# Subtracting the block means from V on VectorE ahead of the mix, in place of a second matmul per column

## The chip, the cores and the metric

The kernel runs on one core of one Trainium2 chip. The metric is the device time of one execution in microseconds (us); less is better. A profile is one execution; its span is some 2 us shorter than the device time of the same execution. Engines are named as in the profile: PE is TensorE's matmuls, PEld its weight loads, DVE VectorE, ACT ScalarE, POOL GpSimd, SP SyncE. Names in the profile's lines: pm and pf are PSUM tiles; vst is V of the first mix as loaded, vcx V in the order that a mix reads, vbn its mean, bdv the block-diagonal P, vsf the mixed V; qr is a copy of q; un is the layer norm's result, w1sb and w2sb the MLP's weights, hr its hidden layer, and u what goes out.

## The reference, cut to what matters

The code is written out in short here, not word for word.

```python
# attention over 4 batches x 8 heads, 768 positions in 8 blocks of 96, head width 64
P = sort_net                               # 8 x 8 for each (batch, head)
for _ in range(5):
    P = ...                                # exp, rows and columns normalised in turn
k_sorted = einsum('bhij,bhjcd->bhicd', P, k_blocks)
v_sorted = einsum('bhij,bhjcd->bhicd', P, v_blocks)     # "the mix" of this text
attn = softmax(q_blocks @ k_sorted^T / 8)
x = attn @ v_sorted                        # then 2D Fourier mix, layer norm,
...                                        # and an MLP 512 -> 2048 -> 512 with two residuals
```

The kernel works with V less its mean over the 96 rows of a block. The mean goes through a small path of its own, in float32. Batches 0 and 1 are mixed together (the first mix), batches 2 and 3 together (the second mix).

## The kernel before

The rows of V lie on partitions, one for each (batch, head, block), 128 for two batches. For every one of the 64 columns of the head, one matmul has that column of V (96 rows and padding) as weights and a block-diagonal copy of P as the moving matrix. A second matmul into the same PSUM column takes off the mean.

```python
def v_sort(n):                      # first mix only: V in the order that the mix needs
    nc.vector.tensor_copy(vcx[...4 * n:4 * n + 4], vst[:, 24 * n:24 * n + 24, :]...)
    op("DVE", 0.6)

def vb_make(t, src):                # the mean, and its negative in 16 bits
    ...
    vbn[t] = const.tile([128, D], F16, name=f"vbn{t}")
    nc.vector.tensor_scalar(vbn[t], vb[:, 0, :], -1.0, None, op0=ALU.mult)
    ...

def v_mix(t, n):                    # n = 0..15: four columns
    bd = bdv16[t].rearrange("p g i -> p (g i)")
    ps = pm([128, 4, 128])
    for dd in range(4):
        d = 4 * n + dd
        nc.tensor.matmul(ps[:, dd, :], vcx[:, :, d], bd, start=True, stop=False)
        nc.tensor.matmul(ps[:, dd, :], vbn[t][:, d:d + 1].broadcast_to([128, 128]),
                         bd, start=False, stop=True)
    t = op("PE", 0.46)
    evac(vsb[0:96, :, 4 * n:4 * n + 4], ps[0:96]..., t, 512)   # PSUM to SBUF, on ACT or DVE
```

`op(engine, us)` computes nothing on the chip. It keeps an estimated clock for each engine while the program is being written, and these estimates decide which of several streams (attention, mix, Fourier transform, layer norm, MLP) writes its next piece, and whether ACT or DVE evacuates. A scheduler of the build then moves instructions within windows (64 instructions on PE, 12 on DVE and on ACT). So a figure given to `op` changes the order of instructions, and at times which of the two engines evacuates, but never what is computed.

The softmax here doesn't subtract the row's maximum and nothing guards it: scores larger than these inputs give would overflow.

Of the kernel before, what the change touches and what calls it, by code (L numbers as in the profile page):

```python
# [10 lines left out]
F16 = mybir.dt.float16  # L11
I32 = mybir.dt.int32
AF = mybir.ActivationFunctionType
ALU = mybir.AluOpType
# [6 lines left out]
D = 64  # L21
# [79 lines left out]
def kernel(  # L101
# [10 lines left out]
    nc = tc.nc  # L112
    cn = {n: nc.inline_tensor(a, name="k_" + n) for n, a in _consts().items()}

    const = ctx.enter_context(tc.tile_pool(name="const", bufs=1))
# [12 lines left out]
    def pm(shape, dtype=F32):  # L128
        cnt[0] += 1
        return pml.tile(shape, dtype, tag="pm", name=f"pm{cnt[0]}")  # L130

    def wt(shape, dtype, tag, bufs, nm=None):
        cnt[0] += 1
        return work.tile(shape, dtype, tag=tag, bufs=bufs,
                         name=f"{nm or tag}{cnt[0]}")
# [18 lines left out]
    def op(e, dur, after=0.0):  # L154
        t = max(clk[e], after) + dur
        clk[e] = t
        return t + LAT
# [5 lines left out]
    def evac(dst, src, after, n):  # L163
        da, dv = 0.22 + n / 1200.0, 0.15 + n / 960.0
        e = pick(after, da, dv)
        if e == "ACT":
            nc.scalar.copy(dst, src)  # L167
            return op(e, da, after)
        nc.vector.tensor_copy(dst, src)
        return op(e, dv, after)  # L170
# [41 lines left out]
    vcx = const.tile([128, 128, D], F16, name="vcx")  # L212
# [3 lines left out]
    def load_v(t):  # L216
        for g in range(2):
            start(nc.gpsimd.dma_start(
                vcx[:, 48 * g:48 * g + 48, :].rearrange(
                    "p (c r) d -> p c (r d)", r=3),  # L220
                vv[128 * t:128 * t + 128, :, g, :]))
# [15 lines left out]
    for n in range(NKS):  # L237
        t = const.tile([128, NB, 128], F16, name=f"ksb{n}")
# [19 lines left out]
    pwt = pw.rearrange("p i j -> p j i")  # L258

    def v_sort(n):  # L260
        nc.vector.tensor_copy(
            vcx[:, 0:BLK, :].rearrange("p (g c r) d -> p g c (r d)", g=2, r=3)[
                :, :, 4 * n:4 * n + 4],
            vst[:, 24 * n:24 * n + 24, :].rearrange(
                "p (c g r) d -> p g c (r d)", g=2, r=3))
        op("DVE", 0.6)

    def v_mean(psm, n, src=vcx):
        nc.tensor.matmul(  # L269
            psm.rearrange("p c d -> p (c d)"), idh,  # L270
            src[:, 8 * n:8 * n + 8, :].rearrange("p c d -> p (c d)"),
            start=(n == 0), stop=(n == 11))
        op("PE", 0.22)
# [3 lines left out]
    def q_copy(b, hp, after=0.0):  # L277
        hf, hl = divmod(hp, 2)
        q16 = qk["q", b, hf]
        qr = wt([128, 6, 2, D], F16, "qr", 2)  # L280
        nc.vector.tensor_copy(
            qr, q16[:, 2 * hl:2 * hl + 2].rearrange("p h r d -> p r h d"))
        qrs[b, hp] = (qr, op("DVE", 0.35, after))

    ph = []
    for it in range(5):
        if it == 0:
# [3 lines left out]
                op=ALU.subtract)  # L291
# [28 lines left out]
    for c in range(4):  # L320
        w = nc.gpsimd.dma_start(w1sb[:, c, :], w1v[:, c, :])
# [23 lines left out]
    psm = pm([128, 8, D])  # L345
# [5 lines left out]
    t = wt([128, H, NB, 16], F16, "bdk", 2)  # L351
    for hh in range(2):
# [5 lines left out]
            op=ALU.mult)  # L358
# [6 lines left out]
    def kq(b, hp):  # L365
        hf, hl = divmod(hp, 2)
        k16 = qk["k", b, hf]
        ks = ksb[kcnt[0] % NKS]
        kcnt[0] += 1
        for half in range(2):  # L370
            ps = pf([128, 3, 128])
            for r3 in range(3):
                r = 3 * half + r3
                for h2 in range(2):
                    nc.tensor.matmul(  # L375
                        ps[64 * h2:64 * h2 + 64, r3, :],
                        k16[:, 2 * hl + h2, r, :],
                        bdk[b][:, 2 * hp + h2].rearrange("p i c -> p (i c)"))
            t = op("PE", 0.2)
            t1 = evac(ks[:, :, 48 * half:48 * half + 48].rearrange(  # L380
                "p i (c r) -> p i c r", r=3),
                ps.rearrange("p r (i c) -> p i c r", c=16), t, 384)
        qr, tq = qrs[b, hp]
        ps = pf([128, 6, 128], F16)
        for r in range(6):
            nc.tensor.matmul(ps[:, r, :], qr[:, r].rearrange("p h d -> p (h d)"),  # L386
                             idh, is_transpose=True)
        t = op("PE", 0.35, tq)
        qt = wt([128, 6, 128], F16, "qt", 3)
        nc.vector.tensor_copy(qt, ps)  # L390
        t2 = op("DVE", 0.55, t)
        return ks, qt, max(t1, t2)
# [70 lines left out]
    vbn = {}  # L463

    def bdv_make():
        psv = pm([128, NB, 32])
        for i in range(NB):
            nc.tensor.matmul(psv[:, i, :], pv[:, i, :], idf[0:32, 0:32])
        for t in range(2):
            b32 = const.tile([128, 16, NB], F32, name=f"bdv32_{t}")  # L470
            nc.vector.tensor_tensor(
                b32, psv[:, :, 16 * t:16 * t + 16].rearrange("p i g -> p g i"),
                maskg[:, :, None].broadcast_to([128, 16, NB]), op=ALU.mult)
            b16 = const.tile([128, 16, NB], F16, name=f"bdv16_{t}")
            nc.scalar.copy(b16, b32)
            bdv32.append(b32)
            bdv16.append(b16)

    def vb_make(t, src):
        vb = const.tile([128, 2, D], F32, name=f"vb{t}")  # L480
        nc.vector.tensor_reduce(vb[:, 0, :], src.rearrange("p c d -> p d c"),
                                axis=AX.X, op=ALU.add)
        nc.vector.tensor_scalar(vb[:, 0, :], vb[:, 0, :], 1.0 / BLK, None,
                                op0=ALU.mult)
        vbn[t] = const.tile([128, D], F16, name=f"vbn{t}")
        nc.vector.tensor_scalar(vbn[t], vb[:, 0, :], -1.0, None, op0=ALU.mult)
        nc.vector.tensor_copy(vb[:, 1, :], vb[:, 0, :])
        vbs[t] = vb

    def v_mix(t, n):  # L490
        bd = bdv16[t].rearrange("p g i -> p (g i)")
        ps = pm([128, 4, 128])
        for dd in range(4):
            d = 4 * n + dd
            nc.tensor.matmul(ps[:, dd, :], vcx[:, :, d], bd, start=True,  # L495
                             stop=False)
            nc.tensor.matmul(ps[:, dd, :],  # L497
                             vbn[t][:, d:d + 1].broadcast_to([128, 128]),
                             bd, start=False, stop=True)
        t = op("PE", 0.46)  # L500
        evac(vsb[0:96, :, 4 * n:4 * n + 4],
             ps[0:96].rearrange("p d g -> p g d"), t, 512)

# [368 lines left out]
    def v1_gen():  # L872
        load_v(1)
        while (0, 0) not in uns:
            yield None
        ps = pm([128, 8, D])
        for n in range(12):
            v_mean(ps, n)
        vb_make(1, ps)
        op("DVE", 0.9, clk["PE"])  # L880
        while 1 not in attnd:
            yield None
        for n in range(16):
            v_mix(1, n)
            yield clk["PE"] + 0.6
        vmixed[0] = True
# [29 lines left out]
    def sc(kk):  # L916
        es = new_es()
        t0 = scores(*kk[:2], 0, es)
        t1 = scores(*kk[:2], 1, es)
        return kk + (es, [max(a, c) for a, c in zip(t0, t1)])  # L920
# [2 lines left out]
    k0 = {0: kq(0, 0)}  # L923
    for n in range(6, 12):
        v_mean(psm, n, vst)
    for n in range(4):
        v_sort(n)
    k0[0] = sc(k0[0])
    bdv_make()
    q_copy(0, 1)  # L930
    k0[1] = kq(0, 1)
    nc.scalar.copy(tkh, psk)
    vb_make(0, psm)
    k0[1] = sc(k0[1])
    load_qk(1, 0)
    for n in range(16):
        v_mix(0, n)
# [14 lines left out]
    add(1, a_gen())  # L952
    add(2, attn_gen(k0))
    add(3, v1_gen())
    add(4, mlp_gen())
    with ExitStack() as later:
# [42 lines left out]
```

## Time and profile before

The time before is 323.6 us (median of 3 runs, 322.8 to 323.98). From the page of the profile, the line of PE: busy us, share of the span, instructions.

```profile
PE 290.4 (90%) x2444; PEld 181.8 (57%) x2444; DVE 203.0 (63%) x454; ACT 122.6 (38%) x254; POOL 40.1 (12%) x73
```

PE is the busiest engine, but the average hides three stages. The chain that ended last shows the first one (columns: start us, us, what):

```profile
22.08 28.77 DMA q<-in_q_dram
51.56 1.15 PE pf L444 x12
```

One load, of q for batch 1, lies across the whole first mix (24 to 35 us) and releases the work at 51 us. Next, the busy time of each engine in stretches of the span:

```profile
core 0: us, PE busy (x) PEld busy (x) DVE busy (x) ACT busy (x) POOL busy (x), PEclk, DMA share, GB/s
80.00:86.00 6.00, 5.13 (x78) 4.31 (x72) 3.86 (x12) 4.37 (x10) 0.00 (x0) 1.00 0.83 128
86.00:100.00 14.00, 13.07 (x170) 10.46 (x169) 13.70 (x28) 12.11 (x25) 4.75 (x6) 1.00 0.04 4
100.00:110.00 10.00, 9.74 (x133) 8.41 (x133) 4.15 (x12) 9.93 (x22) 0.00 (x0) 1.00 0.51 78
110.00:125.00 15.00, 14.75 (x188) 10.49 (x186) 10.72 (x32) 9.92 (x24) 1.49 (x2) 1.00 0.41 61
125.00:314.00 189.00, 188.53 (x1201) 104.12 (x1200) 110.08 (x221) 45.09 (x91) 11.19 (x24) 1.00 0.15 43
```

The second mix runs from 82 to 107 us. From 86 to 100 us PE stands still for 0.9 of 14 us and DVE is busy for 13.7; ACT is busy for 12.1, and for 9.9 of the 10 us that follow. After 125 us PE is full: whatever PE saves before, or loses, appears at the end.

The groups that the change touches (line, engine, operation, operands, shape, count, busy us, mean ns, idle before them):

```profile
L495 PE MATMUL pm<-bdv,vcx 128*128 128x128 f16 x128 | 21.9, 267 | 1.0 <-DMA vcx<-k_dtab 0.5 <-ACT vsf L167 0.5
L497 PE MATMUL pm<-bdv,vbn 128*128 128x128 f16 x128 | 21.6, 237 | 0.0
L636 DVE TENSOR_TENSOR pmt<-r 128x1536 f16<-128x1536 f16 x8 | 7.4, 952 | 0.0
L261 DVE COPY vcx<-vst 128x1536 f16<-128x1536 f16 x4 | 2.0, 552 | 0.0
```

The mean ns of a matmul is its latency, and matmuls overlap. What one costs is read from the timeline, as the distance of the starts (columns: start us, us, engine, line, operation):

```profile
89.04 0.22 PE L497 MATMUL pm<-bdv,vbn 128*128 128x128 f16 x1
89.10 0.25 PE L495 MATMUL pm<-bdv,vcx 128*128 128x128 f16 x1
89.19 0.22 PE L497 MATMUL pm<-bdv,vbn 128*128 128x128 f16 x1
89.25 0.26 PE L495 MATMUL pm<-bdv,vcx 128*128 128x128 f16 x1
```

A pair starts every 0.148 us. The matmul with the column of V is followed after 0.09 us, the one with the mean after 0.06.

### The profile page before, as it was taken

To read this page: it belongs to the slowest core of one execution; us is meant where nothing else is said; L and a number is where in the kernel's file an instruction comes from. 1 tells how busy PE (TensorE), PEld (TensorE's weight loads), DVE (VectorE), ACT (ScalarE), POOL (GpSimd) and SP (SyncE) were. 2 spreads that over 40 slices of the span, in tenths; PEclk is the share of its full clock that TensorE was granted. 3 is DMA by queue.
4 is the path that set the end of the run, shared out by engine and by line. 5 is a ranking of instruction groups with operands and counts; after the bars stand their busy time and mean duration, and the time that the engine had idled before them with its cause. 6 is when DMAs were issued, how large, how long until landed. Compare 5 with 4: busy or idle time off the path is not lost.

```text
span 321.6 us, 5938 instructions
## 1 busy us (share of the span) xinstructions
PE 290.4 (90%) x2444; PEld 181.8 (57%) x2444; DVE 203.0 (63%) x454; ACT 122.6 (38%) x254; POOL 40.1 (12%) x73
## 2 busy tenths in 40 slices
PE   0389974699899999999999999999999999999995
PEld 0169853466777776455455656554664564554642
DVE  6795686888795656466495667644943662872831
ACT  2266481568789963012048843210460120110000
POOL 8320051013122010010003000100020010010000
PEclk9986995599999999999999999999999999999999
DMA  8999979971506070102111100021021120121002
GB/s 126 209 290 219 207 122 208 175 103 19 91 3 98 2 100 15 65 34 51 62 48 35 19 33 35 33 51 65 33 51 59 41 51 33 66 48 68 33 2 98
DMA packets 30131, 24.90 MB, mean 77 GB/s; under 512 B 15028, under 2 KB 25780, under 8 KB 30102
## 3 DMA queue, kind: packets, MB, share of 16 engines
q0 software_dynamic: 15552, 13.63, 27.3%
q1 hardware_dynamic: 14552, 10.89, 11.2%
q8 instruction: 19, 0.31, 0.4%
q14 instruction: 8, 0.07, 0.1%
HBM read 29.10 MB, written 6.29 MB: 110 GB/s over the span
## 4 chain that ended last, share of the span: by engine, by line
PE 70%; DMA 9%; ACT 9%; DVE 6%; issue 3%; POOL 2%; POOLq 0%; ACTq 0%
PE pm L802 26%; PE pm L785 24%; DMA q<-in_q_dram 9%; PE pf L749 7%; PE pf L444 4%; ACT ex L408 2%; PE pf L666 2%; PE pf L752 2%; PE pf L400 2%; ACT eb L424 1%; PE pf L375 1%; PE pf L386 1%; ACT vsf L167 1%; ACT un L714 1%; DVE eb L234 1%
## 5 line engine op out<-in xcount | busy, mean ns | idle before, releaser
L785 PE MATMUL pm<-ut,w1sb 128*128 128x384 f16 x512 | 92.5, 327 | 0.0
L802 PE MATMUL pm<-w2sb,hr 128*128 128x512 f16 x384 | 86.8, 379 | 0.0
L785 PEld LDWEIGHTS <-w1sb 128*128 128x128 f16 x512 | 49.8, 100 | 32.9 <-issue 1.2
L802 PEld LDWEIGHTS <-hr 128*128 128x128 f16 x384 | 37.3, 99 | 42.7
L794 ACT ACTIVATE hr<-pm 128x384 f16<-128x384 f32 x47 | 22.9, 493 | 99.1 <-PE pm L785 99.0
L790 DVE TENSOR_SCALAR hr<-pm 128x384 f16<-128x384 f32 x81 | 44.8, 555 | 20.7 <-PE pm L785 17.1
L811 DVE TENSOR_TENSOR u<-pm,u 128x512 f32<-128x512 f32 x24 | 16.5, 687 | 40.9 <-PE pm L802 40.9
L408 ACT ACTIVATE ex<-pf 96x384 f32<-96x384 f32 x64 | 28.2, 489 | 11.8 <-PE pf L400 11.6
L444 PE MATMUL pf<-vsf,eb 97*128 97x96 f16 x384 | 21.3, 211 | 5.5 <-DVE eb L421 4.5
L714 ACT ACTIVATE un<-u,nm,ny 128x512 f16<-128x512 f32 x20 | 15.6, 809 | 25.3 <-POOL nm L702 19.5
L698 POOL TENSOR_SCALAR mv<-mv 128x3 f32<-128x3 f32 x8 | 3.3, 417 | 173.5 <-DVE mv L760 173.5
L444 PEld LDWEIGHTS <-eb 97*128 97x128 f16 x384 | 19.5, 100 | 8.3 <-DVE eb L421 4.6
L424 ACT ACTIVATE eb<-ex,negone 96x384 f16<-96x384 f32 x38 | 23.1, 622 | 0.3
L495 PE MATMUL pm<-bdv,vcx 128*128 128x128 f16 x128 | 21.9, 267 | 1.0 <-DMA vcx<-k_dtab 0.5
L756 DVE SCALAR_TENSOR_TENSOR u<-r,pf 128x512 f32<-128x512 f16 x24 | 16.3, 681 | 9.5 <-DMA out_dram<-u 5.7
L497 PE MATMUL pm<-bdv,vbn 128*128 128x128 f16 x128 | 21.6, 237 | 0.0
L495 PEld LDWEIGHTS <-vcx 128*128 128x128 f16 x128 | 20.1, 173 | 1.3 <-issue 0.9
L497 PEld LDWEIGHTS <-vbn 128*128 128x128 f16 x128 | 17.4, 136 | 0.7 <-issue 0.7
L456 DVE TENSOR_TENSOR r<-pf,rz 128x384 f16<-128x384 f32 x32 | 17.1, 551 | 0.5
L759 DVE BATCH_NORM_STATS2 st<-u 128x6 f32<-128x512 f32 x24 | 16.5, 688 | 0.3
L167 ACT CAST vsf<-pm 96x512 f16<-96x512 f32 x18 | 14.3, 813 | 4.3 <-PE pm L497 4.0
L269 PE MATMUL pm<-vst,pack 128*128 128x512 f16 x12 | 4.2, 501 | 12.2 <-DMA vst<-in_v_dram 12.2
(103 smaller groups left out, 327.5 us busy)
## 6 DMA issues: line engine op xcount, KB each, us to landing
out_dram<-u SPq DMA_DIRECT2D x24, 256.0 KB, 2.0
k<-in_k_dram POOLq DMA_DIRECT2D x8, 384.0 KB, 8.2
q<-in_q_dram POOLq DMA_DIRECT2D x8, 384.0 KB, 9.4
w1sb<-in_moe_w_ch_dram POOLq DMA_DIRECT2D x4, 512.0 KB, 19.6
w2sb<-in_moe_w_ch_dram POOLq DMA_DIRECT2D x4, 512.0 KB, 25.1
vst<-in_v_dram POOLq DMA_DIRECT2D x2, 768.0 KB, 10.7
vcx<-in_v_dram POOLq DMA_DIRECT2D x2, 768.0 KB, 22.7
cs<-k_cs SPq DMA_DIRECT2D x1, 579.0 KB, 13.0
```

The costliest lines, as they stand in the source:

```text
L167: nc.scalar.copy(dst, src)
L408: nc.scalar.activation(ex.rearrange("p j (c r) -> p j c r", r=6), pss[h2][0:96].rearrange("p j (r c) -> p j c r", c=16), AF.Exp, scale=SCALE)
L424: nc.scalar.activation(ed, src, AF.Identity, bias=negone[0:96])
L444: nc.tensor.matmul(po[:, 65 * T:65 * T + 96], e[:, S * g + 256 * tt + 128 * n: S * g + 256 * tt + 128 * n + 128], vsf[:, vi:vi + 96], star ...
L495: nc.tensor.matmul(ps[:, dd, :], vcx[:, :, d], bd, start=True, stop=False)
L497: nc.tensor.matmul(ps[:, dd, :], vbn[t][:, d:d + 1].broadcast_to([128, 128]), bd, start=False, stop=True)
L714: nc.scalar.activation(un, ul[tt], AF.Identity, scale=y[:, tt:tt + 1], bias=nm[:, tt:tt + 1])
L749: nc.tensor.matmul(ps[:, c % 2::2], lh, dtab[:, c, :], start=(c == 0), stop=False, skip_group_check=True)
L785: nc.tensor.matmul(ps, w1sb[:, c, 128 * fc:128 * fc + 128], ut[:, c, :], start=(c == 0), stop=(c == 3))
L790: nc.vector.tensor_scalar(hr[:, fc, :], ps, 0.0, None, op0=ALU.max)
L794: nc.scalar.activation(hr[:, fc, :], ps, AF.Relu)
L802: nc.tensor.matmul(ps, hr[:, fc, 128 * tt:128 * tt + 128], w2sb[:, fc, :], start=(fc == 0), stop=(fc == 15))
```

## The change

The mean is taken off on VectorE. In the first mix the sort copy becomes a subtraction; in the second, four subtractions in place stand ahead of the mix. One matmul per column stays. The figures given to `op` change with it. In the opening sequence the subtractions have to follow the mean, so its order changes too.

```diff
--- before.py
+++ after.py
@@ -258,12 +258,25 @@
     pwt = pw.rearrange("p i j -> p j i")
 
     def v_sort(n):
-        nc.vector.tensor_copy(
+        nc.vector.tensor_tensor(
             vcx[:, 0:BLK, :].rearrange("p (g c r) d -> p g c (r d)", g=2, r=3)[
                 :, :, 4 * n:4 * n + 4],
             vst[:, 24 * n:24 * n + 24, :].rearrange(
-                "p (c g r) d -> p g c (r d)", g=2, r=3))
-        op("DVE", 0.6)
+                "p (c g r) d -> p g c (r d)", g=2, r=3),
+            vm3(0)[:, None, None, :].broadcast_to([128, 2, 4, 3 * D]),
+            op=ALU.subtract)
+        op("DVE", 0.9)
+
+    def v_center(n):
+        w = vcx[:, 24 * n:24 * n + 24, :].rearrange(
+            "p (c r) d -> p c (r d)", r=3)
+        nc.vector.tensor_tensor(
+            w, w, vm3(1)[:, None, :].broadcast_to([128, 8, 3 * D]),
+            op=ALU.subtract)
+        op("DVE", 0.9)
+
+    def vm3(t):
+        return vbn[t].rearrange("p r d -> p (r d)")
 
     def v_mean(psm, n, src=vcx):
         nc.tensor.matmul(
@@ -482,8 +495,9 @@
                                 axis=AX.X, op=ALU.add)
         nc.vector.tensor_scalar(vb[:, 0, :], vb[:, 0, :], 1.0 / BLK, None,
                                 op0=ALU.mult)
-        vbn[t] = const.tile([128, D], F16, name=f"vbn{t}")
-        nc.vector.tensor_scalar(vbn[t], vb[:, 0, :], -1.0, None, op0=ALU.mult)
+        vbn[t] = const.tile([128, 3, D], F16, name=f"vbn{t}")
+        nc.vector.tensor_copy(
+            vbn[t], vb[:, 0:1, :].broadcast_to([128, 3, D]))
         nc.vector.tensor_copy(vb[:, 1, :], vb[:, 0, :])
         vbs[t] = vb
 
@@ -492,12 +506,8 @@
         ps = pm([128, 4, 128])
         for dd in range(4):
             d = 4 * n + dd
-            nc.tensor.matmul(ps[:, dd, :], vcx[:, :, d], bd, start=True,
-                             stop=False)
-            nc.tensor.matmul(ps[:, dd, :],
-                             vbn[t][:, d:d + 1].broadcast_to([128, 128]),
-                             bd, start=False, stop=True)
-        t = op("PE", 0.46)
+            nc.tensor.matmul(ps[:, dd, :], vcx[:, :, d], bd)
+        t = op("PE", 0.25)
         evac(vsb[0:96, :, 4 * n:4 * n + 4],
              ps[0:96].rearrange("p d g -> p g d"), t, 512)
 
@@ -878,6 +888,8 @@
             v_mean(ps, n)
         vb_make(1, ps)
         op("DVE", 0.9, clk["PE"])
+        for n in range(4):
+            v_center(n)
         while 1 not in attnd:
             yield None
         for n in range(16):
@@ -923,14 +935,16 @@
     k0 = {0: kq(0, 0)}
     for n in range(6, 12):
         v_mean(psm, n, vst)
-    for n in range(4):
-        v_sort(n)
+    vb_make(0, psm)
     k0[0] = sc(k0[0])
     bdv_make()
+    for n in range(2):
+        v_sort(n)
     q_copy(0, 1)
     k0[1] = kq(0, 1)
     nc.scalar.copy(tkh, psk)
-    vb_make(0, psm)
+    for n in range(2, 4):
+        v_sort(n)
     k0[1] = sc(k0[1])
     load_qk(1, 0)
     for n in range(16):
```

## The prediction

> **What bounds the kernel now.** TensorE is busy 90% (page), but stages differ.
> (a) To 51 us the loads decide: in the chain of waits one piece of 28.8 us, the load of q for batch 1, lands at 50.9 us; DVE idles 4.0 us before it (waits, qr copy). The first mix (24 to 35 us) lies inside, with about 4 us of slack.
> (b) From 80 to 110 us (second mix) all three engines are full: by windows PE is busy 13.1 and DVE 13.7 of 14 us from 86 to 100, ACT 13.6 of 14 from 94 to 108.
> (c) From 125 to 318 us PE is busy 192.4 of 193 us: PE work saved, or idle added, before this shows in full at the end.
>
> **What the change does.** It removes 128 PE matmuls (64 per mix). By timeline a pair starts every 0.148 us at full clock, 0.213 at half clock (24 to 29 us). The Trainium skill ("TensorE: Matmul & The Clock Gate", Back-to-back issue gap and Part 1) gives 107 ns cold and 56 warm for one such matmul. The trace agrees cold; 0.148 is above two warm ones, so I estimate 0.06 to 0.1 us for the strided V load that stays. Saved: some 4 us of PE in each mix (3 to 5.5).
>
> It adds DVE work. The four sort copies (552 ns each, 128x1536 fp16) become subtractions; a tensor_tensor of that size takes 952 ns (pmt group). The skill ("VectorE: DVE Perf Modes", Mode 4×_2P) says tensor_tensor cannot use the fourfold mode; the two times agree. Four in-place subtractions come before the second mix: +3.5 us pipelined. The 16 vsf evacuations per mix stay at 0.8 us over two engines: no mix group below about 0.41 us, against 0.6 now.
>
> **Order.** DVE's built order is unchanged between the first mix and 79 us, with the waiting qr copy in place. The first mix starts about 1.5 us later (subtractions wait for the mean), takes 7 instead of 11 us, and its gain is swallowed by the wait for q: worth 0.
> In the second the subtractions stand between the mean (80.6 us) and the first mix matmul, among eb copies that PE's attention matmuls need. I expect the mix to start near 86.5 instead of 82, with about 2 us of new PE idle. DVE is then 1 to 2 us behind in a stage already full, and two vsf evacuations and some hr move to the full ACT. Most of the saved PE time turns into waits. Both orders join again near 138 us.
>
> **Time.** 4 saved, minus 2 idle at the start, minus about 1 more: -1 us. I predict 322.3 us, 80% range 318.5 to 326. Faster by over 2% 0.06, within 2% 0.91, slower by over 2% 0.03.
>
> **What would show it.** Chain: q still lands near 51 us. Groups: no vbn matmuls; subtractions 0.9 to 1.0 us each. Timeline: first second-mix matmul near 86 us; PE idle from 80 to 110 us up from 2.1 to 4 us or more; the first w2sb matmuls 0 to 2 us earlier than now (124.4); the tail unchanged.
>
> **What would make it wrong.** If q or V land sooner in the early stretch, the gain is 2 to 4 us larger. If subtractions run at one element per cycle (estimate 1.6 us each), DVE falls 3 us further behind: slower. If mlp work fills the stage, the full 4 to 5 us are won.

## The result, and the profile after

The time after is 320.16 us (median of 4 runs, 320.0 to 320.3), against 323.52 us for the kernel before (322.8 to 323.98). The ratio is 0.9896, with a 95% interval of 0.9882 to 0.991: 1.0% less time, which counts as the same at the threshold of 2%. Ratios in this text are taken from runs of both kernels in the same rounds; they need not be the ratio of the medians that are quoted.

The line of PE on the page after, and the same part of the chain:

```profile
PE 283.4 (89%) x2316; PEld 174.3 (55%) x2316; DVE 205.3 (64%) x453; ACT 124.6 (39%) x259; POOL 39.5 (12%) x73
```

```profile
23.44 27.57 DMA q<-in_q_dram
51.72 1.15 PE pf L457 x12
```

128 matmuls and 7 us of PE's busy time are gone, but the load of q still releases the work, 0.16 us later than before. The windows after:

```profile
80.00:86.00 6.00, 4.57 (x73) 3.54 (x69) 5.93 (x13) 4.65 (x10) 0.00 (x0) 1.00 0.86 130
86.00:100.00 14.00, 13.19 (x144) 10.30 (x143) 12.73 (x27) 12.91 (x26) 2.52 (x4) 1.00 0.01 2
100.00:110.00 10.00, 10.00 (x109) 7.49 (x107) 6.81 (x21) 9.95 (x24) 1.62 (x2) 1.00 0.57 80
110.00:125.00 15.00, 15.00 (x185) 10.29 (x183) 8.31 (x21) 9.88 (x24) 1.48 (x2) 1.00 0.43 63
125.00:314.00 189.00, 188.53 (x1218) 104.55 (x1215) 111.22 (x224) 45.15 (x91) 11.21 (x24) 1.00 0.16 46
```

Summed over the first four rows, PE's idle time is 2.31 us before and 2.24 after. The new idle time that the prediction expected isn't there: 0.6 us more before 86 us, and 0.6 less from 86 to 100. (From 80 to 110 us, where it looked for 4 us or more, it is 2.05 before and 2.24 after.) The groups after:

```profile
L509 PE MATMUL pm<-bdv,vcx 128*128 128x128 f16 x128 | 15.5, 268 | 2.4 <-issue 1.0 <-DVE vsf L169 0.6 <-DVE vcx L273 0.4
L273 DVE TENSOR_TENSOR vcx<-vcx,vbn 128x1536 f16<-128x1536 f16 x4 | 3.8, 942 | 0.0
L261 DVE TENSOR_TENSOR vcx<-vst,vbn 128x1536 f16<-128x1536 f16 x4 | 3.6, 947 | 0.0
```

The subtractions take 942 and 947 ns, as the tensor_tensor of the same shape did before. And the timeline of PE after, at the start of the second mix:

```profile
86.48 0.57 PE L509 MATMUL pm<-bdv,vcx 128*128 128x128 f16 x4 [0.43 <-DVE vcx L273]
86.89 0.81 PE L795 MATMUL pm<-ut,w1sb 128*128 128x384 f16 x4
87.54 0.49 PE L509 MATMUL pm<-bdv,vcx 128*128 128x128 f16 x4
...
90.66 1.24 PE L509 MATMUL pm<-bdv,vcx 128*128 128x128 f16 x12
```

The second mix starts 4.5 us later (81.94 before), as predicted, but PE works on other matmuls until then, and matmuls of the MLP (w1sb) fill the gaps between the groups of four. From a group of 12 (1.24 us) and one of 4 (0.49), the distance of two mix matmuls is about 0.75/8 = 0.094 us; in weight loads, twelve take 1.26 us, with starts 0.097 us apart. Against the pair's 0.148 that saves 0.051 us, times 64 columns 3.3 us in each mix.

To say where the gain arises, I cut the span at two marks that every version has: the end of the matmuls that sum the second mean, and the fourth of the output additions of the MLP. Here is the last group of the first mark and then the second mark, before and after:

```profile
78.09 1.24 PE L269 MATMUL pm<-vcx,pack 128*128 128x512 f16 x5
...
156.51 0.69 DVE L811 TENSOR_TENSOR u<-pm,u 128x512 f32<-128x512 f32 x1 [4.62 <-PE pm L802]
```

```profile
78.25 1.24 PE L282 MATMUL pm<-vcx,pack 128*128 128x512 f16 x5
...
153.20 0.69 DVE L821 TENSOR_TENSOR u<-pm,u 128x512 f32<-128x512 f32 x1 [4.62 <-PE pm L812]
```

The busy times between the marks, before and after:

```profile
79.33:156.51 77.18, 74.88 (x738) 51.14 (x736) 47.74 (x109) 40.05 (x83) 7.80 (x12) 1.00 0.28 50
79.49:153.20 73.71, 71.47 (x674) 47.87 (x671) 49.44 (x111) 40.94 (x86) 7.18 (x12) 1.00 0.30 52
```

So the three parts of the span are 79.33, 77.18 and 165.09 us before, and 79.49, 73.71 and 165.10 after. The whole gain arises in the middle part. The busy time of PE there fell from 74.88 to 71.47 us, by 3.4, which agrees with the 3.3 us from the distances of the matmuls. Counted in the same traces from each start to the next start or idle time, the second mix's own matmuls take 10.12 us before and 6.67 after, 3.45 less; all other matmuls of this part together take the same to 0.1 us, though single groups differ by up to 0.4.

### The profile page after: what moved, and what is told of

Same layout as the page of the kernel before. It is cut to its first block, busy times and chain, and to the rows that moved or that the text cites. A ratio compares the mean times of both kernels' runs of the same rounds, so it can differ in the third digit from the quotient of the medians.

```text
span 318.3 us, 5693 instructions
## 1 busy us (share of the span) xinstructions
PE 283.4 (89%) x2316; PEld 174.3 (55%) x2316; DVE 205.3 (64%) x453; ACT 124.6 (39%) x259; POOL 39.5 (12%) x73
## 4 chain that ended last, share of the span: by engine, by line
PE 77%; DMA 11%; DVE 5%; ACT 4%; issue 1%; POOL 1%; ACTq 0%; POOLq 0%
PE pm L812 26%; PE pm L795 25%; DMA q<-in_q_dram 9%; PE pf L759 6%; PE pf L457 4%; DMA vst<-in_v_dram 3%; PE pf L676 3%; PE pm L282 2%; PE pf L413 2%; PE pf L388 2%; PE pm L509 2%; PE pf L399 2%; PE pf L762 2%; ACT ex L421 1%; DVE vcx L273 1%
## 5 line engine op out<-in xcount | busy, mean ns | idle before, releaser
L804 ACT ACTIVATE hr<-pm 128x384 f16<-128x384 f32 x50 | 24.8, 500 | 93.2 <-PE pm L795 93.2
L800 DVE TENSOR_SCALAR hr<-pm 128x384 f16<-128x384 f32 x78 | 43.1, 554 | 20.4 <-PE pm L795 16.8
L437 ACT ACTIVATE eb<-ex,negone 96x384 f16<-96x384 f32 x39 | 24.1, 629 | 0.4
L167 ACT CAST vsf<-pm 96x512 f16<-96x512 f32 x20 | 16.4, 834 | 3.3 <-PE pm L509 3.2
L509 PE MATMUL pm<-bdv,vcx 128*128 128x128 f16 x128 | 15.5, 268 | 2.4 <-issue 1.0
L509 PEld LDWEIGHTS <-vcx 128*128 128x128 f16 x128 | 14.3, 192 | 4.1 <-issue 2.9
L167 ACT CAST ksb<-pf 128x384 f16<-128x384 f32 x23 | 10.6, 491 | 10.4 <-PE pf L388 10.4
L413 PE MATMUL pf<-qt,ksb 64*128 64x96 f16 x256 | 12.8, 213 | 1.4 <-DVE qt L403 0.6
```

The source lines that it names most:

```text
L167: nc.scalar.copy(dst, src)
L413: nc.tensor.matmul(pss[h2][:, j, :], ks[rows, 4 * g + j], qt[rows, :, cc])
L437: nc.scalar.activation(ed, src, AF.Identity, bias=negone[0:96])
L509: nc.tensor.matmul(ps[:, dd, :], vcx[:, :, d], bd)
L800: nc.vector.tensor_scalar(hr[:, fc, :], ps, 0.0, None, op0=ALU.max)
L804: nc.scalar.activation(hr[:, fc, :], ps, AF.Relu)
```

## The experiments

All kernels below are timed against the kernel before in the same rounds. "Same order" means that the built instruction streams of PE, DVE and ACT are the same, instruction for instruction, from the second mean on. The three parts are those of the profiled run, with the marks from above. The first part differs by 0.5 us between the two runs of the full change (79.49 and 78.99), so smaller differences in that column show nothing. I show the sums first; the single experiments follow.

| kernel | time, median | ratio [95%] | to the 2nd mean | middle | rest |
|---|---|---|---|---|---|
| before | 323.52 | 1 | 79.33 | 77.18 | 165.09 |
| full change | 320.16 | 0.9896 [0.9882, 0.991] | 79.49 | 73.71 | 165.10 |
| full change, again | 320.36 | 0.9891 [0.9876, 0.9906] | 78.99 | 73.66 | 165.15 |
| second mix only | 325.17 | 1.0047 [1.0027, 1.0067] | 79.36 | 76.45 | 166.39 |
| second mix only, in the full change's order | 322.47 | 0.9955 [0.9943, 0.9968] | 79.40 | 73.63 | 167.67 |
| first mix only | 325.75 | 1.0069 [1.005, 1.0088] | 79.40 | 77.16 | 166.64 |
| before, told 0.25 | 322.11 | 0.9946 [0.9933, 0.9958] | 79.58 | 75.60 | 165.12 |
| full change, told 1.0 | 319.56 | 0.986 [0.9843, 0.9878] | 79.32 | 73.44 | 165.14 |
| full, without the in-place subtractions (wrong) | 317.66 | 0.9822 [0.9801, 0.9843] | 78.36 | 72.02 | 165.12 |
| before, with the in-place subtractions (wrong) | 328.87 | 1.0157 [1.0134, 1.0179] | 80.12 | 83.48 | 165.10 |
| full, contiguous weights (wrong) | 319.70 | 0.9884 [0.9868, 0.9899] | 78.93 | 73.26 | 165.11 |
| before, early load | 322.58 | 0.9968 [0.9955, 0.9982] | 78.01 | 77.22 | 165.07 |
| full change, early load | 318.30 | 0.9841 [0.9824, 0.9858] | 77.57 | 73.69 | 165.04 |
| full change, early load, told 1.0 | 319.19 | 0.9863 [0.9849, 0.9876] | 78.59 | 73.46 | 165.15 |

The starting theory (A) was: the gain is the PE work taken out of the second mix, the first mix is worth nothing, and the change falls into parts that can be measured one by one. Its rivals: (B) the gain comes from the first mix or from the early stretch; (C) the gain depends on the order that the build finds for each program, so that the parts don't add up.

### Only the second mix changed

```diff
 # against the kernel before, cut; v_center is that of the full change
+            if t == 1:
+                nc.tensor.matmul(ps[:, dd, :], vcx[:, :, d], bd)
+                continue
...
-        t = op("PE", 0.46)
+        t = op("PE", 0.25 if t == 1 else 0.46)
...
+        for n in range(4):
+            v_center(n)
```

> The change in the second mix alone; the first mix keeps its pairs of matmuls and its plain sort copies. Theory A (the whole gain is PE work taken out of the second mix, 64 times 0.148 minus 0.097 us = 3.3 us, and the four subtractions are hidden): 320.2 us, ratio to before 0.990, the same as the full change. Rival B (the first mix or the early stretch gives a part): between 321 and 323 us.

It is 0.5% slower than before, where theory A had the whole gain. The middle part took 76.45 us, 2.7 more than in the full change, with the very same instructions in it. PE is idle for 4.33 us of it instead of 2.24, and busy for 72.12 instead of 71.47. Most of the idle time is at one place (timeline of PE; in brackets the idle time and what ended it; then the window of the stage):

```profile
90.52 0.50 PE L510 MATMUL pm<-bdv,vcx 128*128 128x128 f16 x4
92.75 0.40 PE L748 MATMUL pf<-pack,un 128*128 128x128 f16 x4 [1.73 <-ACT un L731]
```

```profile
86.00:100.00 14.00, 11.41 (x127) 8.98 (x128) 11.91 (x26) 11.33 (x23) 2.95 (x5) 1.00 0.01 2
```

PE finishes a group of four mix matmuls and then stands for 1.7 us, since the next instruction in its built order transposes the layer norm's result `un`, which ACT hasn't written yet. In the full change the same place has 12 mix matmuls and some of the MLP. Here the expected idle time of the prediction is real: 2.59 of 14 us. The last part grew by 1.3 us as well, of which 1.1 are a wait as in the next experiment.

### Only the first mix changed

```diff
 # against the full change, cut; the second mix has pairs of matmuls, as before
-        for n in range(4):
-            v_center(n)
```

> The change in the first mix alone; the second keeps its pairs. Theory A: 323.5 us, ratio 1.000 within 0.002; the first mix starts 2.5 us later (near 26.4 us), ends at 35.0 us as before, and the load of q lands near 51 us as before. Rival B: 1 us or more faster than before.

The middle part is 77.16 us, that of before, whose built order it shares; the first mark is 0.07 us later. So the first mix with its change is worth nothing in this kernel, which settles rival B for the first mix. (It did not run when expected: it went from 27.98 to 36.73 us, and q was copied at 50.94.) Yet the time is 0.7% worse than before. All of that lies in the last part, where the order is that of before too (timeline of DVE):

```profile
163.37 0.69 DVE L777 SCALAR_TENSOR_TENSOR u<-r,pf 128x512 f32<-128x512 f16 x1 [1.40 <-DMA out_dram<-u]
```

VectorE waits 1.4 us for a buffer of `u` that an output store still reads. That store took 3.7 us from issue to landing; the median of the stores whose landing the profile has (13 of 24) is 2.0, before and here. The same slow store, at about the same place, is in the second-mix kernel (3.4 us) and in its reordered form below (3.3 us). The longer last part goes with their longer times, so it isn't an accident of one profile. What sets these stores apart is in the list of DMAs: one packet of the kind `instruction`, of 16 KB, moves within their time. The queue's line and the store's line (KB, us to landing) of this kernel from 159.5 to 163.5 us, and then the store's line of the kernel before from 159 to 163 us, where there is no such packet:

```profile
q8 instruction: 1, 0.02, 2.2%
out_dram<-u SPq DMA_DIRECT2D x1, 256.0 KB, 3.7
out_dram<-u SPq DMA_DIRECT2D x1, 256.0 KB, 2.0
```

The other two have it too. Worked out from the packets of all 14 traces: a store that meets such a packet 0.3 to 1.2 us after its issue has its last data packet 2.3 to 3.4 us after the issue, every other store at most 2.0 us. Each kernel has such a store, but elsewhere it costs little: in the kernel before it is the one issued at 193.8 us, and no wait follows. That the instruction packet slows the store is thus likely, though no run moved it alone. Why it falls on the store at 159 us in just these three is not shown; they share a count of PE matmuls (2380, against 2444 or 2316).

### The full change without its in-place subtractions

This result is wrong (relative error 0.023): it shows what the four subtractions cost.

```diff
-        for n in range(4):
-            v_center(n)
```

> The full change without the four subtractions before the second mix: wrong values on purpose, it only shows what the subtractions cost. Theory A (hidden): 319.6 to 320.3 us, at most 0.5 us under the full change. The view of my prediction (about 2 us of new idle at the start of the second mix and about 1 us of DVE delay): about 317 us.

The middle part is 1.7 us shorter than in the full change. Another 1.1 us came before the first mark, in which the subtractions don't lie, so the difference of the times (2.5 us between the medians) overstates them. The built order of the middle differs as well (in the trace, 285 of the 1723 PE matmuls from the second mean on stand elsewhere), so 1.7 us is what the subtractions cost together with the order, not by themselves; 0.5 of it is idle time of PE (1.74 us against 2.24). The time came near the 317 us that the prediction's view gave, and not near theory A's: the subtractions can't be called hidden.

### The kernel before with the in-place subtractions added

Also wrong: VectorE takes the mean off, and the second matmul of each pair, whose weights have the other sign here, adds it again.

```diff
+        for n in range(4):
+            v_center(n)        # pairs of matmuls stay
```

> The kernel before with the four subtractions added ahead of the second mix, and all pairs of matmuls kept: wrong values on purpose (the mean is taken off once by DVE and the pair's second weights have the opposite sign). It loads DVE without relieving PE. Theory A: 323.5 to 324.3 us. The view of my prediction: 326 us or more. Rival C (the gain comes from the order that the scheduler builds around the subtractions, not from the removed matmuls): 321 us or less.

The middle part took 83.48 us, 6.3 more than before, of which 4.1 (83.48 less 79.36 busy) are PE's idle time. But the order differs here too, the granted clock of PE fell to 0.84 between 80 and 100 us, and the profiled run was the slowest of its five (330.5). It fits the subtractions being in the way where PE work isn't saved, as the prediction's view had it (326 us or more); it gives no price for them.

After these four, theory A had fallen in its form: two halves, each slower than before, make a whole that is faster. The next four test theory C.

### The full change again

No edit; it ran in later rounds.

> The full change once more, on the chip of the other three. All theories: about 320.2 us, ratio 0.990; in the trace 101.5 us from the first attention matmul after the q load to the fourth output addition, against 105.0 before.

The gain repeats: 0.9891 against 0.9896. The middle part differs by 0.05 us. How far a profile may be trusted here shows in the table: four kernels with the full change's order from the second mean on (the full change twice, once more with the early load, and the one that follows) have 73.63 to 73.71 us, and three with the order of before 77.16 to 77.22.

### Second mix only, in the full change's order

Against "second mix only", one figure told to the scheduler is another. No instruction changes.

```diff
     def v_sort(n):
         nc.vector.tensor_copy(...)
-        op("DVE", 0.6)
+        op("DVE", 0.9)
```

> The second-mix-only kernel with one build-time number changed: the duration that the scheduler is told for a sort copy is 0.9 instead of 0.6 us. No instruction is added or removed, but from the second mean on the built order on every engine becomes that of the full change. Theory C (the gain is PE work removed from the second mix, and whether it shows depends on the order that the build found): the stretch from the q load to the fourth output addition goes from 104.4 to 101.5 us, and the time from about 325.2 to about 321 us, unless the slow store of the output at 158 us comes back too (then 322.5). Rival (the first mix gives part of the gain): no change against second_only, 324 to 325.5 us.

With this figure the order from the second mean on is that of the full change, and the middle part goes from 76.45 to 73.63 us. The timeline and window at the place of the long wait:

```profile
90.57 1.25 PE L510 MATMUL pm<-bdv,vcx 128*128 128x128 f16 x12
92.01 0.81 PE L802 MATMUL pm<-ut,w1sb 128*128 128x384 f16 x4 [0.19 <-ACT vsf L167]
92.66 0.49 PE L510 MATMUL pm<-bdv,vcx 128*128 128x128 f16 x4
93.30 0.40 PE L748 MATMUL pf<-pack,un 128*128 128x128 f16 x4 [0.16 <-ACT un L731]
```

```profile
86.00:100.00 14.00, 13.26 (x144) 10.43 (x144) 12.75 (x27) 13.01 (x27) 2.52 (x4) 1.00 0.01 2
```

The wait for `un` shrank from 1.7 us to 0.2, since 12 mix matmuls, MLP matmuls and four more of the mix now stand before it. With the same instructions, order alone is worth 2.8 us in the middle part: 2.1 of PE's idle time (4.33 to 2.22) and 0.7 of its busy time. And the change in the second mix alone, in the right order, gives the whole 3.5 us there. The last part, though, is 2.6 us longer (167.67), so that its time is 322.47: VectorE waits 3.1 us for output stores there, against 1.3 in the full change, 1.1 of it for one slow store as above (the expectation allowed for it, with 322.5 us). Another 0.7 follow at 223.9 us, after a store issued at 221.1 that meets an instruction packet as well. The rest of the 2.6 us I have not traced to single waits.

### Before and after with other figures for the scheduler

```diff
 # before, told 0.25
-        t = op("PE", 0.46)
+        t = op("PE", 0.25)
 # full change, told 1.0, in v_center
-        op("DVE", 0.9)
+        op("DVE", 1.0)
```

> The kernel before with one build-time number changed: a mix group is told to the scheduler with 0.25 instead of 0.46 us of PE, as in the full change. Same instructions, 524 PE matmuls in other places. Theory C: between 321.5 and 326 us. Rival D (the new duration alone, by the order it leads to, gives the 3.4 us): 320.2 us.

> The full change with one build-time number changed: the duration told for a subtraction before the second mix is 1.0 instead of 0.9 us. Same instructions, 78 PE matmuls in other places. Theory C: the time moves by 1 to 3 us in either direction, most likely up to 321 to 323 us. Rival (the order is worth nothing): 320.2 us within 0.5.

The kernel before gains 0.5% by the order alone; its middle part is 1.6 us shorter. Only 0.2 us of that is idle time of PE (2.08 against 2.30); its busy time fell from 74.88 to 73.52 us with the same matmuls, so the order also moves what they add up to. The full change gains some 0.3% more than it has (ratio 0.986 against 0.9891 in the same rounds; the intervals just overlap), where the expectation had rather looked for a loss. So half of the full change's gain can be had without the change, by luck of the order: against the kernel before told 0.25, the full change saves 1.9 us in the middle part, not 3.5 (2.2 with each in its better order). What the removed matmuls are worth by themselves thus depends on the order they are taken from, and a difference of 1% between two programs that this scheduler ordered is no proof of what an instruction costs.

### Loading q of batch 1 earlier, before and after

The prediction took the wait for q to swallow the first mix's gain. Here the first half of k and q of batch 1 is loaded ahead of w1, into a buffer that is free.

```diff
+    qk10 = wt([128, 2, 4, 6, D], F16, "hr", 2, "qk10")
+    for n_, (src, nm) in enumerate(((k, "k"), (q, "q"))):
+        start(nc.gpsimd.dma_start(qk10[:, n_]..., src[1, 0:4, :, :]...))
+        qk[nm, 1, 0] = qk10[:, n_]
 ...
-    load_qk(1, 0)
```

> The kernel before, with the first half of k and q of batch 1 loaded ahead of w1 into a buffer that is free, so that the copies of q at about 51 us should wait for no load; from the second mean on the built order of TensorE, VectorE and ScalarE is that of before. Theory 'the load of q ends the first stretch': the wait of VectorE for q (4.0 us before) goes, and the fourth output addition comes 2 to 4 us earlier than 156.5 us. Rival 'TensorE or ScalarE work of the first stretch is as long as the load': the wait moves elsewhere and that addition moves by under 1 us. If the early load delays V or w1 instead, it is slower.

> The full change with the same earlier load; built order from the second mean on as in the full change. The prediction said that the first mix's gain is swallowed by the wait for q and that the whole gain would be 2 to 4 us larger if q landed sooner: then before with the early load minus this kernel is 5 to 7 us (at the fourth output addition and in time). Rival, from the traces: the first mix starts 2.5 us later and so ends when it ended before, so it is worth nothing with or without the wait for q: the difference stays at 3 to 3.5 us, and this kernel comes near 317 us.

Both kernels gain, and only ahead of the first mark: 1.3 us for the kernel before, 1.9 for the full change. The wait at 51 us is gone, but the next load of q takes its place. From the waits of VectorE, before and then after, each with the early load (columns: who waits for what, us in total, times, longest):

```profile
DVE qr L287 <- DMA q<-in_q_dram: 2.0, 1, 2.0
```

```profile
DVE qr L300 <- DMA q<-in_q_dram: 4.0, 1, 4.0
```

It lands at 61.0 us in the one and at 60.6 in the other. In this pair the full change does seem to bring the work forward: VectorE comes to the wait at 56.6 us instead of 59.0 (the landing less the wait). Then it waits 2.0 us longer, and 0.4 us are left at the second mean, no more than two runs of one kernel differ there. That is what the prediction's mechanism, swallowed by the wait for q, would look like; but its inference that the gain would be 2 to 4 us larger with an earlier q was not borne out by moving this load. At the fourth output addition the pair differs by 4.0 us, between the two expectations (5 to 7, and 3 to 3.5), and the earlier load by itself moved that addition by 1.3 us, between 2 to 4 and under 1. The middle parts don't change (77.22 and 73.69). With 318.30 us, 1.6% below before, the full change with the early load is the fastest correct kernel.

### The early load and the other figure together

```diff
 # full change with early load
-        op("DVE", 0.9)         # in v_center
+        op("DVE", 1.0)
```

> The full change with the earlier load and the build's scheduler told 1.0 instead of 0.9 us for each subtraction of the second mix, which gave 0.8 us in time without the earlier load. If the two gains lie in different stretches they add: some 0.5 to 1 us below the full change with the earlier load. If not, it is the same within 0.3%.

The two gains did not add. The middle part did get 0.2 us shorter, as without the early load, but the second mean ended 1.0 us later and the time is 0.9 us worse (the intervals of the two ratios just overlap). Figures for a scheduler that help one version need not help its neighbour.

### Contiguous weights

In the full change a column of V is one value in 64, that is, 128 bytes apart. The Trainium skill ("SBUF — State Buffer", Door 1: The DMA port swizzle) says that reads which cross to a new line of 16 bytes with every element pay for it. This kernel, wrong (relative error 0.30), takes 128 values that lie side by side.

```diff
-            nc.tensor.matmul(ps[:, dd, :], vcx[:, :, d], bd)
+            w = vcx[:, :, d]
+            if t == 1:
+                w = vcx[:, 2 * (d % 48):2 * (d % 48) + 2, :].rearrange("p c d -> p (c d)")
+            nc.tensor.matmul(ps[:, dd, :], w, bd)
```

> Wrong on purpose. The full change with the weights of the second mix taken as 128 values that lie side by side instead of one in 64 (the numbers mixed are then the wrong ones); instructions and counts are the same, the built order differs in 138 TensorE matmuls. Theory 'the stride of the weight load sets the 0.097 us of a mix matmul': the mix matmuls go at near 0.06 us, TensorE is about 2.5 us less busy, and the output additions come up to 2.5 us earlier. Rival 'the switch of the PSUM column or the 128 columns of the moving matrix set it': it stays at 0.09 to 0.10 us.

The groups of the second mix between 82 and 106 us, in the full change (run again) and then with contiguous weights:

```profile
L509 PE MATMUL pm<-bdv,vcx 128*128 128x128 f16 x64 | 7.9, 253 | 0.4 <-DVE vcx L273 0.4
L509 PEld LDWEIGHTS <-vcx 128*128 128x128 f16 x64 | 7.5, 196 | 1.3 <-DVE vcx L273 0.6 <-issue 0.2
```

```profile
L513 PE MATMUL pm<-bdv,vcx 128*128 128x128 f16 x64 | 6.0, 219 | 0.4 <-ACT hr L808 0.3
L513 PEld LDWEIGHTS <-vcx 128*128 128x128 f16 x64 | 4.3, 97 | 2.0 <-issue 0.9
```

A weight load takes 97 ns instead of 196, and the mix is 1.9 us shorter for PE. A group of four takes 0.39 us instead of 0.50. So the stride does set a large part of what is left of a mix matmul, as the skill's page has it for reads in general. But the middle part fell by only 0.4 us, with another order:

```profile
86.00:100.00 14.00, 12.11 (x147) 8.19 (x146) 12.69 (x27) 13.64 (x27) 2.31 (x5) 1.00 0.01 2
```

Now PE idles 1.9 of 14 us while ACT is busy 13.6, and most of its waits in this stretch are for results of ACT (0.8 us for evacuations of the mix, 0.3 for the MLP's `hr`, 0.6 for `un`). Saving still more PE time in the mix is thus not worth much in this order: the saved time does turn into waits here.

## Why the prediction was right or wrong

The time was right in kind: 320.16 us within the range of 318.5 to 326, and within 2% of before. The gain was 3.4 us where 1.3 were predicted, so the width of the range carried the forecast and not its sum.

- **First mix worth 0: right**, and shown by the kernel with only that change (first mark 0.07 us later, middle part the same). Its shape was not as predicted: it started 2.5 us later instead of 1.5 (26.45 against 23.94), and took 8.65 us instead of 7, so it ended when it ended before (35.1 against 35.2). In that run there was nothing for the wait for q to swallow. But its place moves between runs: in the full change again it went from 29.16 to 37.81 us, VectorE's wait for q was 1.0 instead of 4.1, and the second mean was no later. So the slack ahead of q is real; with the early load the next load of q took it up.
- **Durations of the subtractions, start of the second mix, tail: right.** 942 and 947 ns for an expected 0.9 to 1.0 us; 86.48 us for "near 86"; 165.10 us for the last part, against 165.09. (The first w2sb matmul was to come 0 to 2 us earlier; it came 5.7 earlier, at 118.58 instead of 124.27.) The Trainium skill ("VectorE: DVE Perf Modes", Why `tensor_tensor` can't do 2×_2P or 4×) gives the reason that a subtraction costs more than the copy; the trace has 947 against 552 ns.
- **Saved PE time: 4 us in each mix predicted, 3.3 to 3.5 measured in the second.** A strided matmul alone costs 0.097 us, at the upper end of the estimate of 0.06 to 0.1. The contiguous weights show the larger part of it: the stride of the weights.
- **"With about 2 us of new PE idle ... about 1 more": this is the step that failed.** PE's idle time in the stage was 2.31 us before and 2.24 after. The later start added no idle time over the kernel before, as attention and MLP matmuls filled it. In the sum "4 saved, minus 2, minus 1", the measured terms are 3.3, 0 and 0 against the kernel before. Against the same kernel without its subtractions there is a loss of 1.7 us, with another order, of which 0.5 are idle time: less than the 3 that the prediction took off, but not nothing.
- **"Most of the saved PE time turns into waits": wrong for this built order, right for others.** With the same second-mix instructions in another order, the middle part gained 0.7 us instead of 3.5 and PE idled 2.6 of 14 us. The prediction named the alternative ("if mlp work fills the stage"), and this is what happened; but the "full 4 to 5 us" that it attached to it were 3.5.
- What stays open: the price of the four subtractions by themselves (1.7 us in the middle part, together with another order), how the 3.5 us divide between the removed matmuls and the order, why an instruction packet meets the store at 159 us in just three kernels, and whether some order would win more than the 73.44 us that was the best of the middle part in a correct kernel.

## What to carry to other kernels

When a scheduler orders the program, a change of instructions is a change of order too, and here order alone was worth 1.6 to 2.8 us in two pairs of kernels, against 3.5 for the change with its order. Undo or redo single parts only with a look at the built order, and compare stretches between marks in kernels whose order is the same: there they agreed within 0.1 us, while the times of the halves pointed the wrong way. Work added to an engine that is off the critical path costs little only if the engine that is on it has other work in its order at that place; read that from the timeline at the wait, not from shares of busy time. And time saved ahead of a wait for a load doesn't come back by moving that load alone, if the next load then ends the wait.

## What the Trainium skill lacked or had wrong

- "TensorE: Matmul & The Clock Gate" (Weight-path perf modes) names the read pattern of the fast weight load as "packed or strided". It gives no time for a stride: 128 weights of 16 bits took 97 ns side by side and 196 ns at a stride of 64 elements.
- The same page (Back-to-back issue gap) gives about 56 ns for the isolated gap and about 81 ns sustained for 128 columns with weight loads. Here the matmul that weighted the mean was followed after 0.06 us, and strided ones started 0.094 to 0.097 us apart; the sustained figure fitted neither.
- "DMA: Bandwidth & Descriptors" (Anatomy of one DMA) gives, for DMAs issued from GpSimd, about 2.0 us plus the bytes over 436 GB/s; by that, my estimate for an output store of 256 KB is 2.6 us. These stores are issued from SyncE, and their median was 2.0 us. No page says that a store can take longer beside a packet of instructions: 3.3 to 3.7 us in three kernels, which cost up to 1.4 us at one wait.
- No page says how to compare kernels whose order a scheduler of the build decides: figures told to it moved the time by 0.5% in one pair and 0.9% in another, with no instruction changed.
